# Linear attention and a four-expert mixture on one core: w1 in another row order, all its casts on POOL, and batches 0 and 1 in another order

## The chip, the cores and the metric

The kernel runs on one core of one Trainium2 chip. The time is that of the device, in microseconds (us), for one launch with inputs and outputs in HBM. Each kernel is launched several times and the median counts.

## The reference

All inputs are fp32. With q, k, v of shape [8 batches, 8 heads, 576 rows, 64], phi(x) = elu(x) + 1:

```python
q_p, k_p = (phi(q), phi(k))
kv = np.einsum('bhsd,bhse->bhde', k_p, v)
z = np.sum(k_p, axis=2)
num = np.einsum('bhsd,bhde->bhse', q_p, kv)
den = np.einsum('bhsd,bhd->bhs', q_p, z)[..., None] + 1e-06
x = (num / den).transpose(0, 2, 1, 3).reshape(4608, 512)
p = domain_probs / (domain_probs.sum(-1, keepdims=True) + 1e-09)    # [4608, 4]
for e in range(4):                      # w1[e]: [512, 1024], w2[e]: [1024, 512]
    h = np.maximum(x @ w1[e], 0.0)
    out += p[:, e:e + 1] * (h @ w2[e])
```

## The kernel before

The engines are PE (TensorE: matmuls and transposes), DVE (VectorE), ACT (ScalarE), POOL (GpSimd) and SP (SyncE, which issues nearly all DMAs). The order of the work on every engine, and of SP's DMAs, is written out by hand (`manual_schedule`): an engine does its instructions in the order in which the Python code emits them. SP's DMAs use eight semaphores in turn, so each issue waits until the eighth DMA before it has landed.

**Attention.** A batch is two head groups g of four heads. `load` brings one group of k, q or v (576 KB) into a `stage` tile; `exp` (ACT), `lin` and `phi` (DVE) make phi; `vcast` makes v fp16 (`vp`); `kv` multiplies phi(k) with v, and ACT copies the product to `kvz`; `qtr` transposes phi(q) on PE and `qcopy` brings it to `qT` (`qdma` does the same by a transposing DMA); `numden` multiplies and divides, giving `xs`; `xtr` transposes `xs` on PE and copies it to `xT` (`xdma`: by DMAs). `xT` holds x transposed, fp16, with its rows in the order (g, hh, a, d): of a group's four heads, head number 2a + hh.

**Mixture.** `moe_first` does the first 512 rows of x, expert by expert: eight products `ph` with w1 (L414, evicted by ACT, L421), then four products `py` with w2 (L427, scaled and added by DVE, L437 and L439). `moe_tile(i)`, i = 2 to 17, does 256 rows each; its second product takes seven products instead of eight from sums and differences of w2's quarters (`make_T` prepares them; `pB` holds the probabilities along the rows). In `moe_first` the work of batch 1, the loading of the later experts and the preparation hang on numbered slots, 12 for each expert: `at(h, 12 * e + fj, ...)` stands ahead of `ph` number fj, `12 * e + 8 + ns` ahead of `py` number ns.

**Weights.** w1 and w2 are loaded as fp32 in pieces of 512 KB into tiles that have another use later (`homes` gives their tags) and cast to fp16. A piece of w1 has 128 successive rows on the partitions, twice. `xT` wants another row order in which halves of 64 rows change places, so w1 is cast in pieces of 64 partitions by 512: the straight half on POOL (`cast_w1` with a = hh), the crossing half on ACT or DVE (`cross_w1`). Of w2's four pieces POOL casts two and DVE two.

**Probabilities.** `load_probs` has its two DMAs issued by POOL, behind the casts of w1(0) and w2(0) there; `norm_probs` normalizes (DVE), `turn_probs` transposes and writes them to DRAM (`p_rows`), from where `pB` is read.

**Order at the start.** SP: k, q, v of batch 0, then w1(0), w2(0), w1(1); in the slots w2(1), w1(2), w2(2), w1(3), batch 1's k, v, q, w2(3). Batch 0 goes through phi of k for both groups, then of q, before the products begin; `warmup` puts matmuls without use on PE.

Of the kernel before, what the change touches and what calls it, by code (L numbers as in the profile page):

```python
# [21 lines left out]
def kernel(  # L22
# [10 lines left out]
    nc = tc.nc  # L33

    B, H, S, D = q.shape
    N, E = moe_domain_probs.shape
    _, Dm, F = moe_w1.shape
# [9 lines left out]
    P = 128  # L47
    HP = P // 2
    CB = S // HP
    G = H // 4  # L50
    DC = Dm // P
    FC = F // P
    NT = 512
# [9 lines left out]
    CS = 5  # L63
# [14 lines left out]
    w1_sb = pw.tile([P, E, DC, F], FP16, tag="w1")  # L78
    w2_sb = pw.tile([P, E, FC, Dm], FP16, tag="w2")
    xT = pc.tile([P, DC, RC * HP], FP16, tag="xT")  # L80
    w1_src = moe_w1.rearrange("e (dc p) f -> e p dc f", p=P)
    w2_src = moe_w2.rearrange("e (fc p) d -> e p fc d", p=P)
    NTP = N // P
    p_raw = pc.tile([P, (2 * NTP + 1) * E], FP32, tag="praw")
# [23 lines left out]
    class Batch:  # L108
# [91 lines left out]
        def numden(self, g, part, where=None):  # L200

            c0, c1 = ((0, 6), (6, CB))[part]
            if part == 0:
                self.xs[g] = att([P, CB, 2, D], "xs")
            if where:
                nd = ppm.tile([P, NT], FP32, tag=where, bufs=3, name="nd").rearrange(
                    "p (k n) -> p k n", k=1
                )
            else:
                nd = ppa.tile([P, 2, NT], FP32, tag="aps", bufs=1, name="nd")  # L210
            for c in range(c0, c1):
                i = c - c0
                for hh in range(2):
                    rows = slice(hh * HP, (hh + 1) * HP)
                    nc.tensor.matmul(  # L215
                        out=nd[rows, i // 3, (i % 3) * 2 * DE : (i % 3 + 1) * 2 * DE],
                        lhsT=self.qT[g][:, c, rows],
                        rhs=self.kvz[g][:, hh, :],
                        start=True,
                        stop=True,  # L220
                    )
            nb = (c1 - c0) // 3
            view = nd[:, 0:nb, 0 : 6 * DE].rearrange("p k (m e) -> p k m e", e=DE)
            rc = pa.tile([P, 2, 6], FP32, tag="rc", bufs=4, name="rc")[:, 0:nb, :]
            nc.vector.tensor_scalar(
                rc, view[:, :, :, D : D + 1].rearrange("p k m o -> p k (m o)"),
                1e-6 * INV, None, AO.add,
            )
            nc.vector.reciprocal(rc, rc)
            nc.vector.tensor_tensor(  # L230
                out=self.xs[g][:, c0:c1, :, :].rearrange(
                    "p (k c) a d -> p k (c a) d", k=nb
                ),
                in0=view[:, :, :, 0:D],
                in1=rc.broadcast_to([P, nb, 6, D]),
                op=AO.mult,
            )
# [45 lines left out]
                    c += n  # L283


    staged = {}
    homes = iter(
        ("Ta",) * 3 + ("Tb",) * 3 + ("S",) * 2
        + ("chain", "pB", "wx") + ("Ta",) * 3 + ("stage",) * 2
        + ("stage",) * 4 + ("Tb",) * 3 + ("S",)  # L290
        + ("S", "chain", "pB", "wx") + ("Tb",) * 3 + ("S",)
    )
    BUFS = {"stage": 6, "Ta": 3, "Tb": 3, "S": 2, "chain": 1, "pB": 1, "wx": 1}

    def wstage(name):
        tag = next(homes)
        return pa.tile([P, 2, NT], FP32, tag=tag, bufs=BUFS[tag], name=name)

    def load_w1(e):
        for fh in range(2):  # L300
            for g in range(2):
                wr = wstage("wr")
                nc.sync.dma_start(
                    out=wr, in_=w1_src[e, :, 2 * g : 2 * g + 2, fh * NT : (fh + 1) * NT]
                )
                staged[1, e, fh, g] = wr
                for i in range(2):
                    cast_w1(e, fh, g, i, i, nc.gpsimd.tensor_copy)

    def cast_w1(e, fh, g, a, hh, copy):  # L310

        copy(
            out=w1_sb[a * HP : (a + 1) * HP, e, 2 * g + hh, fh * NT : (fh + 1) * NT],
            in_=staged[1, e, fh, g][hh * HP : (hh + 1) * HP, a, :],
        )

    def cross_w1(e, fh, copy):
        for g in range(2):
            for i in range(2):
                cast_w1(e, fh, g, i, 1 - i, copy)  # L320

    def load_w2(e):
        for i in range(4):
            wr = wstage("wr")
            nc.sync.dma_start(out=wr, in_=w2_src[e, :, 2 * i : 2 * i + 2, :])
            staged[2, e, i] = wr
            if i % 2 == 0:
                cast_w2(e, i, nc.gpsimd.tensor_copy)

    def cast_w2(e, i, copy):  # L330
        copy(out=w2_sb[:, e, 2 * i : 2 * i + 2, :], in_=staged[2, e, i])

    def load_probs():
        src = moe_domain_probs.rearrange("(b p c) e -> p b (c e)", b=B, c=CB)
        n = 2 * NTP * E
        for hh, at in ((0, E), (1, 0)):
            nc.gpsimd.dma_start(  # L337
                out=p_raw[hh * HP : (hh + 1) * HP, at : at + n].rearrange(
                    "p (b w) -> p b w", b=B
                ),  # L340
                in_=src,
            )
# [230 lines left out]
    def warmup(n, stat=None):  # L573
        pz = ppm.tile([P, NT], FP32, tag="mm", bufs=3, name="pz")
        for _ in range(n):
            nc.tensor.matmul(
                out=pz, lhsT=identh if stat is None else stat, rhs=warm, start=True, stop=True
            )
# [14 lines left out]
    nc.scalar.activation(warm[:, 0:1], identh[:, 0:1], AF.Exp)  # L593

    b0 = Batch(0)
    for src in (k, q, v):
        for g in range(G):
            b0.load(src, g)
    b0.vcast(0, gcopy, CS, CB)
    b0.vcast(1, gcopy, CS, CB)  # L600
    load_w1(0)
    load_w2(0)
    load_probs()
    load_w1(1)

    for g in range(G):
        b0.exp(k, g)
        b0.lin(k, g)
        b0.phi(k, g)
    warmup(6, b0.kp[0][:, 0, :, :].rearrange("p a d -> p (a d)"))  # L610
    b0.exp(q, 0)
    b0.lin(q, 0)
    b0.phi(q, 0)
    b0.exp(q, 1)
    b0.lin(q, 1)
    b0.phi(q, 1)
    b0.qtr(0, ("yy", "yy"))
    b0.vcast(0, scopy, 0, CS)
    b0.qtr(1, ("mm", "mm"))
    b0.kv(0)  # L620
    b0.qcopy(0, 0, vcopy)
    b0.qcopy(0, 1, vcopy)
    b0.vcast(1, vcopy, 0, CS)
    b0.qcopy(1, 0, scopy)
    b0.qcopy(1, 1, vcopy)
    b0.numden(0, 0)
    b0.kv(1, ("yy", "mm"))
    b0.numden(0, 1, "yy")
    cross_w1(0, 0, scopy)
    b0.numden(1, 0)  # L630
    b0.numden(1, 1, "mm")
    warmup(2)
    b0.xtr(0, (scopy, scopy))
    warmup(2)
    b0.xtr(1, (vcopy, scopy), ("yy", "yy"))

    def at(h, s, *fns):
        h.setdefault(s, []).extend(fns)

    def L(f, *args):  # L640
        return lambda: f(*args)
# [1 line left out]
    gps, dve = nc.gpsimd, nc.vector  # L643
    bt = Batch(1)
    h = {}
    at(h, 0, L(load_w2, 1), L(load_w1, 2), L(cross_w1, 0, 1, vcopy))
    at(h, 7, norm_probs)
    at(h, 12, L(load_w2, 2), L(load_w1, 3))
    at(h, 13, *[L(bt.load, s, g) for s in (k, v, q) for g in range(G)])
    at(h, 14, L(bt.vcast, 0, gcopy), L(bt.vcast, 1, gcopy), L(load_w2, 3))  # L650
    at(h, 18, turn_probs)
    for e in range(E):
        for i in (1, 3):
            at(h, 12 * e + 2 * i, L(cast_w2, e, i, vcopy))
    for s, e, fh in ((8, 1, 0), (10, 1, 1), (20, 2, 0), (22, 2, 1)):
        at(h, s, L(cross_w1, e, fh, scopy))
    at(h, 29, L(cross_w1, 3, 0, vcopy))
    at(h, 31, L(cross_w1, 3, 1, vcopy))
    at(h, 32, L(bt.exp, k, 0), L(bt.lin, k, 0))
    at(h, 33, L(bt.exp, k, 1), L(bt.phi, k, 0))  # L660
    at(h, 34, L(bt.lin, k, 1))
    at(h, 35, L(bt.phi, k, 1))
    at(h, 36, L(bt.kv, 0), L(bt.exp, q, 0), L(bt.lin, q, 0))
    at(h, 37, L(bt.phi, q, 0))
    at(h, 38, L(bt.kv, 1), L(bt.exp, q, 1), L(bt.lin, q, 1))
    at(h, 39, L(bt.qtr, 0), L(bt.qcopy, 0, 0, vcopy), L(bt.qcopy, 0, 1, vcopy))
    at(h, 40, L(bt.phi, q, 1), L(load_pB, 2))
    at(h, 42, L(bt.qtr, 1, ("yy", "yy")), L(bt.qcopy, 1, 0, vcopy), L(bt.qcopy, 1, 1, vcopy))
    at(h, 43, L(bt.numden, 0, 0))
    at(h, 44, L(bt.numden, 0, 1, "mm"))  # L670
    at(h, 45, L(bt.numden, 1, 0))
    at(h, 46, L(bt.numden, 1, 1, "mm"), L(bt.xtr, 0, (scopy, scopy)))
    at(h, 47, L(bt.xtr, 1, (scopy, scopy), ("mm", "mm")))
    for s, kind in zip((13, 14, 15, 16), (3, 1, 2, 4)):
        at(h, s, L(make_T, 0, kind, dve))
    at(h, 41, lambda: gcopy(out=after, in_=bt.qp[1][:, 0, 0, 0:1]))
    at(h, 41, *[L(make_T, 1, kind, gps) for kind in (3, 1, 2, 4)])
    at(h, 42, *[L(make_T, 2, kind, gps) for kind in (3, 1, 2, 4)])
    b2 = Batch(2)
    at(h, 48, *[L(b2.load, s, g) for s in (k, q, v) for g in range(G)])  # L680
    moe_first(h)
# [85 lines left out]
```

## Time and profile before

| | us |
|---|---|
| median of 3 runs | 529.11 (528.38 to 529.33) |
| profiled execution | 528.63 |
| its span | 526.9 |
| PE busy | 510.1 |
| DVE, ACT, POOL busy | 324.0, 190.2, 208.8 |
| first `ph` of `moe_first` begins | 19.72 |
| `moe_tile(2)` begins | 82.58 (on the chain of waits: 82.74) |

The profile is of one execution on the chip. Times in it are us from the start of the span, unless marked ns. "Busy" of PE contains pipelined matmuls, so that two of them may overlap. Windows give, for a stretch, each engine's busy time and number of instructions, the granted clock, the share of the 16 DMA engines' time and GB/s. The list of DMA issues gives a transfer's tile and source, its issuing queue, number, size, and the time from the issue to its landing. The granted clock was 0.999 of full speed.

### The profile page before, as it was taken

Reading aid. Unit: us, or ns where it says so; the run is one execution under the profiler, and the core shown is the slowest. Engines: PE = TensorE matmul, PEld = TensorE weight load, DVE = VectorE, ACT = ScalarE, POOL = GpSimd, SP = SyncE. Lnnn points to the kernel's source line nnn. Section 1 sums busy time; section 2 is a strip of 40 time slices with the busy share of each in tenths; the row PEclk is TensorE's granted clock in tenths of the full one; section 3 lists DMA queues with packets and bytes.
Section 4 is the critical chain, followed back from the end, with each engine's and each line's share of the span. In section 5 each row is a group of like instructions: output and inputs, shape, how many; then the busy total and the mean of one; then the engine's idle time right before and its main releaser. Section 6 shows DMA issues by size and latency. Waiting matters only on the chain.

```text
span 526.9 us, 11518 instructions
## 1 busy us (share of the span) xinstructions
PE 510.1 (97%) x4756; PEld 419.9 (80%) x4756; DVE 324.0 (61%) x669; ACT 190.2 (36%) x327; POOL 208.8 (40%) x193
## 2 busy tenths in 40 slices
PE   3889999999999999999999999999999999999996
PEld 1434457888888888888888888888888888888885
DVE  5655976877647674767377746765576545444443
ACT  5767543424341425143523433153413131313130
POOL 3768369324151605051423334241515060606060
PEclk9999999999999999999999999999999999999999
DMA  8999827356554137341923273524143202020301
GB/s 325 406 379 406 317 60 224 148 139 186 135 213 115 47 83 268 83 89 41 309 61 90 63 234 118 96 77 130 33 95 46 81 1 82 2 81 3 78 2 40
DMA packets 65330, 70.97 MB, mean 135 GB/s; under 512 B 31821, under 2 KB 40157, under 8 KB 65277
## 3 DMA queue, kind: packets, MB, share of 16 engines
q1 hardware_dynamic: 65180, 70.08, 42.9%
q8 instruction: 37, 0.61, 0.5%
q0 software_dynamic: 96, 0.15, 0.1%
q14 instruction: 17, 0.13, 0.1%
HBM read 53.62 MB, written 9.51 MB: 120 GB/s over the span
## 4 chain that ended last, share of the span: by engine, by line
PE 93%; DMA 5%; DVE 1%; POOL 0%; SPq 0%; issue 0%; DVEq 0%
PE ph L480 43%; PE px L515 16%; PE py L515 11%; PE pz L515 5%; PE pw L515 5%; PE py L427 4%; PE ph L414 4%; DMA wr<-in_moe_w_dram 2%; PE nd L215 2%; PE pk L167 2%; DMA st<-in_v_dram 2%; DMA p_raw<-in_moe_domain_probs_dram 1%; SPq L117 0%; POOL p_raw L337 0%; PE pq L187 0%; PE px L264 0%
## 5 line engine op out<-in xcount | busy, mean ns | idle before, releaser
L498 POOL TENSOR_TENSOR ga<-hr,pB 128x512 f16<-128x512 f16 x120 | 143.4, 1195 | 272.5 <-ACT hr L497 272.5
L480 PE MATMUL ph<-xT,w_sb 128*128 128x256 f16 x2048 | 232.5, 273 | 0.0
L480 PEld LDWEIGHTS <-w_sb 128*128 128x128 f16 x2048 | 197.4, 98 | 26.1
L492 DVE SCALAR_TENSOR_TENSOR ga<-ph,pB 128x512 f16<-128x512 f32 x136 | 94.0, 692 | 111.8 <-PE ph L480 111.4
L497 ACT ACTIVATE hr<-ph 128x512 f16<-128x512 f32 x120 | 71.6, 597 | 185.3 <-PE ph L480 184.1
L515 PEld LDWEIGHTS <-ga 128*128 128x128 f16 x1280 | 125.2, 98 | 14.5
L515 PEld LDWEIGHTS <-s 128*128 128x128 f16 x512 | 50.0, 98 | 5.9
L135 ACT ACTIVATE ee<-st 128x1152 f16<-128x1152 f32 x32 | 37.0, 1158 | 11.9 <-DMA st<-in_k_dram 10.3
L537 DVE TENSOR_TENSOR s<-ga 128x512 f16<-128x512 f16 x64 | 28.3, 482 | 15.8 <-POOL ga L498 15.8
L515 PE MATMUL pz<-w_sb,ga 128*128 128x256 f16 x256 | 30.6, 273 | 0.0
L515 PE MATMUL pw<-tw,ga 128*128 128x256 f16 x256 | 30.6, 273 | 0.0
L515 PE MATMUL py<-w_sb,s 128*128 128x256 f16 x256 | 30.6, 273 | 0.0
L515 PE MATMUL px<-tw,s 128*128 128x256 f16 x256 | 30.6, 273 | 0.0
L515 PE MATMUL px<-tw,ga 128*128 128x256 f16 x256 | 30.6, 273 | 0.0
L515 PE MATMUL px<-w_sb,ga 128*128 128x256 f16 x256 | 30.6, 273 | 0.0
L515 PE MATMUL py<-w_sb,ga 128*128 128x256 f16 x256 | 30.6, 273 | 0.0
L427 PE MATMUL py<-w_sb,ht 128*128 128x512 f16 x128 | 29.0, 379 | 1.6 <-DVE acc L437 1.6
L414 PE MATMUL ph<-xT,w_sb 128*128 128x512 f16 x128 | 29.2, 379 | 0.3 <-ACT xT L275 0.3
L528 DVE SCALAR_TENSOR_TENSOR res<-px,chain 128x256 f32<-128x256 f32 x32 | 12.1, 420 | 28.1 <-PE px L515 28.1
L142 DVE TENSOR_SCALAR tt<-st 128x1152 f16<-128x1152 f32 x32 | 25.1, 785 | 4.9 <-DMA st<-in_k_dram 4.9
L525 ACT ACTIVATE chain<-px 128x256 f32<-128x256 f32 x32 | 12.3, 383 | 42.2 <-PE px L515 42.2
L149 DVE TENSOR_TENSOR phi<-ee,tt 128x1152 f16<-128x1152 f16 x32 | 24.1, 754 | 2.1 <-ACT ee L135 1.3
(69 smaller groups left out, 376.5 us busy)
## 6 DMA issues: line engine op xcount, KB each, us to landing
wr<-in_moe_w_dram SPq DMA_DIRECT2D x32, 512.0 KB, 11.0
st<-in_k_dram SPq DMA_DIRECT2D x16, 576.0 KB, 6.4
st<-in_q_dram SPq DMA_DIRECT2D x16, 576.0 KB, 5.5
st<-in_v_dram SPq DMA_DIRECT2D x16, 576.0 KB, 8.7
pB<-p_rows SPq DMA_DIRECT2D x16, 512.0 KB, 3.9
out_dram<-res SPq DMA_DIRECT2D x64, 128.0 KB, 2.4
out_dram<-acc SPq DMA_DIRECT2D x8, 128.0 KB, 2.3
xT<-xs SPq DMA_TRANSPOSE x32, 2.6
```

Of the source, the lines that this page charges most:

```text
L135: nc.scalar.activation(self.ee[id(src), g][:, :, c0:c1, :], st[:, :, c0:c1, :], AF.Exp)
L142: nc.vector.tensor_scalar(self.tt[id(src), g][:, :, c0:c1, :], self.st[id(src), g][:, :, c0:c1, :], 0.0, 1.0, AO.max, AO.add,)
L149: nc.vector.tensor_tensor(out=self.dst(src, g)[:, c0:c1, :, :].rearrange("p c a d -> p a c d"), in0=self.ee[id(src), g][:, :, c0:c1, :], i ...
L414: nc.tensor.matmul(out=ph, lhsT=w1_sb[:, e, dc, fj * P : (fj + 1) * P], rhs=xT[:, dc, 0:NT], start=(dc == 0), stop=(dc == DC - 1),)
L427: nc.tensor.matmul(out=py, lhsT=hT[fj // FH][:, fj % FH, ns * P : (ns + 1) * P], rhs=w2_sb[:, e, fj, :], start=(fj == 0), stop=(fj == FC - 1),
L480: nc.tensor.matmul(out=ph[:, f, :], lhsT=w1_sb[:, e, dc, fj * P : (fj + 1) * P], rhs=xT[:, dc, cols], start=(dc == 0), stop=(dc == DC - 1),)
L492: nc.vector.scalar_tensor_tensor(out=to, in0=ph, scalar=0.0, in1=pb, op0=AO.max, op1=AO.mult)
L497: nc.scalar.activation(hr, ph, AF.Relu)
L498: nc.gpsimd.tensor_tensor(out=to, in0=hr, in1=pb, op=AO.mult)
L515: nc.tensor.matmul(out=to, lhsT=sts[e][:, f, :], rhs=movs[e][:, f, :], start=(start and e == 0 and f == 0), stop=(e == E - 1 and f == FH - 1),
L525: nc.scalar.activation(chain[:, n, :], src, AF.Copy, scale=OUTS)
L537: tt(out=S1[e], in0=a21[e], in1=a22[e], op=AO.add)
```

## The change

- w1 is loaded in the row order of `xT`: a transfer brings the 128 rows (a, d) of one (g, hh), with all 1024 columns (512 KB); for expert 0 in two parts of 512 columns (256 KB), the first columns of all four pieces first. The casts are whole (128 partitions), and all on POOL, as are w2's. `cross_w1` goes away.
- `load_probs` goes by SP's queue, between w1(0) and w2(0).
- Batch 0 is loaded in the order k0, q0, v0, q1, k1, v1 and worked off by head group. v's first group is cast whole by POOL.
- Batch 1's k and v are loaded ahead of the last w1, its q behind it. Its second group of q is transposed by DMA (`qdma`) instead of on PE, and its first group of x by DMAs (`xdma`) instead of on PE; its steps stand in somewhat earlier slots, `load_pB(2)` in a later one.
- `make_T` of expert 1 goes from POOL to DVE, in expert 2's slots.

```diff
@@ -200,7 +199,7 @@
         def numden(self, g, part, where=None):
 
             c0, c1 = ((0, 6), (6, CB))[part]
-            if part == 0:
+            if g not in self.xs:
                 self.xs[g] = att([P, CB, 2, D], "xs")
             if where:
                 nd = ppm.tile([P, NT], FP32, tag=where, bufs=3, name="nd").rearrange(
@@ -283,12 +282,11 @@
                     c += n
 
 
-    staged = {}
     homes = iter(
         ("Ta",) * 3 + ("Tb",) * 3 + ("S",) * 2
-        + ("chain", "pB", "wx") + ("Ta",) * 3 + ("stage",) * 2
-        + ("stage",) * 4 + ("Tb",) * 3 + ("S",)
-        + ("S", "chain", "pB", "wx") + ("Tb",) * 3 + ("S",)
+        + ("Ta",) * 3 + ("chain", "stage", "stage", "pB", "wx")
+        + ("Tb",) * 3 + ("S", "S", "chain", "pB", "wx")
+        + ("Tb",) * 3 + ("S", "S", "chain", "pB", "wx")
     )
     BUFS = {"stage": 6, "Ta": 3, "Tb": 3, "S": 2, "chain": 1, "pB": 1, "wx": 1}
 
@@ -296,45 +294,31 @@
         tag = next(homes)
         return pa.tile([P, 2, NT], FP32, tag=tag, bufs=BUFS[tag], name=name)
 
-    def load_w1(e):
-        for fh in range(2):
-            for g in range(2):
-                wr = wstage("wr")
+    w1_rows = moe_w1.rearrange("e (g a hh d) f -> e g hh a d f", g=G, a=2, hh=2)
+
+    def load_w1(e, parts=1):
+
+        n = F // parts
+        wr = [wstage("wr").rearrange("p a f -> p (a f)") for _ in range(DC)]
+        for part in range(parts):
+            cols = slice(part * n, (part + 1) * n)
+            for dc in range(DC):
                 nc.sync.dma_start(
-                    out=wr, in_=w1_src[e, :, 2 * g : 2 * g + 2, fh * NT : (fh + 1) * NT]
+                    out=wr[dc][:, cols], in_=w1_rows[e, dc // 2, dc % 2, :, :, cols]
                 )
-                staged[1, e, fh, g] = wr
-                for i in range(2):
-                    cast_w1(e, fh, g, i, i, nc.gpsimd.tensor_copy)
-
-    def cast_w1(e, fh, g, a, hh, copy):
-
-        copy(
-            out=w1_sb[a * HP : (a + 1) * HP, e, 2 * g + hh, fh * NT : (fh + 1) * NT],
-            in_=staged[1, e, fh, g][hh * HP : (hh + 1) * HP, a, :],
-        )
-
-    def cross_w1(e, fh, copy):
-        for g in range(2):
-            for i in range(2):
-                cast_w1(e, fh, g, i, 1 - i, copy)
+                nc.gpsimd.tensor_copy(out=w1_sb[:, e, dc, cols], in_=wr[dc][:, cols])
 
     def load_w2(e):
         for i in range(4):
             wr = wstage("wr")
             nc.sync.dma_start(out=wr, in_=w2_src[e, :, 2 * i : 2 * i + 2, :])
-            staged[2, e, i] = wr
-            if i % 2 == 0:
-                cast_w2(e, i, nc.gpsimd.tensor_copy)
-
-    def cast_w2(e, i, copy):
-        copy(out=w2_sb[:, e, 2 * i : 2 * i + 2, :], in_=staged[2, e, i])
+            nc.gpsimd.tensor_copy(out=w2_sb[:, e, 2 * i : 2 * i + 2, :], in_=wr)
 
     def load_probs():
         src = moe_domain_probs.rearrange("(b p c) e -> p b (c e)", b=B, c=CB)
         n = 2 * NTP * E
         for hh, at in ((0, E), (1, 0)):
-            nc.gpsimd.dma_start(
+            nc.sync.dma_start(
                 out=p_raw[hh * HP : (hh + 1) * HP, at : at + n].rearrange(
                     "p (b w) -> p b w", b=B
                 ),
@@ -593,46 +577,42 @@
     nc.scalar.activation(warm[:, 0:1], identh[:, 0:1], AF.Exp)
 
     b0 = Batch(0)
-    for src in (k, q, v):
-        for g in range(G):
-            b0.load(src, g)
-    b0.vcast(0, gcopy, CS, CB)
+    for src, g in ((k, 0), (q, 0), (v, 0), (q, 1), (k, 1), (v, 1)):
+        b0.load(src, g)
+    b0.vcast(0, gcopy)
     b0.vcast(1, gcopy, CS, CB)
-    load_w1(0)
+    load_w1(0, 2)
+    load_probs()
     load_w2(0)
-    load_probs()
     load_w1(1)
 
-    for g in range(G):
-        b0.exp(k, g)
-        b0.lin(k, g)
-        b0.phi(k, g)
-    warmup(6, b0.kp[0][:, 0, :, :].rearrange("p a d -> p (a d)"))
-    b0.exp(q, 0)
-    b0.lin(q, 0)
-    b0.phi(q, 0)
-    b0.exp(q, 1)
-    b0.lin(q, 1)
-    b0.phi(q, 1)
-    b0.qtr(0, ("yy", "yy"))
-    b0.vcast(0, scopy, 0, CS)
+    for src, g in ((k, 0), (q, 0), (q, 1)):
+        b0.exp(src, g)
+        b0.lin(src, g)
+        b0.phi(src, g)
+        if g == 0 and src is k:
+            warmup(6, b0.kp[0][:, 0, :, :].rearrange("p a d -> p (a d)"))
+        elif g == 0:
+            b0.qtr(0, ("yy", "yy"))
+            b0.qcopy(0, 0, vcopy)
+            b0.qcopy(0, 1, vcopy)
+    b0.kv(0)
+    b0.exp(k, 1)
+    b0.lin(k, 1)
+    b0.phi(k, 1)
     b0.qtr(1, ("mm", "mm"))
-    b0.kv(0)
-    b0.qcopy(0, 0, vcopy)
-    b0.qcopy(0, 1, vcopy)
-    b0.vcast(1, vcopy, 0, CS)
-    b0.qcopy(1, 0, scopy)
+    b0.qcopy(1, 0, vcopy)
     b0.qcopy(1, 1, vcopy)
+    b0.vcast(1, scopy, 0, CS)
     b0.numden(0, 0)
     b0.kv(1, ("yy", "mm"))
     b0.numden(0, 1, "yy")
-    cross_w1(0, 0, scopy)
+    b0.numden(1, 1, "mm")
     b0.numden(1, 0)
-    b0.numden(1, 1, "mm")
+    warmup(1)
+    b0.xtr(0, (scopy, scopy), ("yy", "yy"))
     warmup(2)
-    b0.xtr(0, (scopy, scopy))
-    warmup(2)
-    b0.xtr(1, (vcopy, scopy), ("yy", "yy"))
+    b0.xtr(1, (scopy, vcopy))
 
     def at(h, s, *fns):
         h.setdefault(s, []).extend(fns)
@@ -643,39 +623,31 @@
     gps, dve = nc.gpsimd, nc.vector
     bt = Batch(1)
     h = {}
-    at(h, 0, L(load_w2, 1), L(load_w1, 2), L(cross_w1, 0, 1, vcopy))
-    at(h, 7, norm_probs)
-    at(h, 12, L(load_w2, 2), L(load_w1, 3))
-    at(h, 13, *[L(bt.load, s, g) for s in (k, v, q) for g in range(G)])
-    at(h, 14, L(bt.vcast, 0, gcopy), L(bt.vcast, 1, gcopy), L(load_w2, 3))
+    at(h, 0, L(load_w2, 1), L(load_w1, 2))
+    at(h, 6, norm_probs)
+    at(h, 12, L(load_w2, 2), *[L(bt.load, s, g) for s in (k, v) for g in range(G)])
+    at(h, 12, L(bt.vcast, 0, gcopy), L(bt.vcast, 1, gcopy))
+    at(h, 13, L(load_w1, 3), *[L(bt.load, q, g) for g in range(G)], L(load_w2, 3))
     at(h, 18, turn_probs)
-    for e in range(E):
-        for i in (1, 3):
-            at(h, 12 * e + 2 * i, L(cast_w2, e, i, vcopy))
-    for s, e, fh in ((8, 1, 0), (10, 1, 1), (20, 2, 0), (22, 2, 1)):
-        at(h, s, L(cross_w1, e, fh, scopy))
-    at(h, 29, L(cross_w1, 3, 0, vcopy))
-    at(h, 31, L(cross_w1, 3, 1, vcopy))
+    for s, kind in enumerate((3, 1, 2, 4)):
+        at(h, 13 + s, L(make_T, 0, kind, dve))
+        at(h, 25 + s, L(make_T, 1, kind, dve))
     at(h, 32, L(bt.exp, k, 0), L(bt.lin, k, 0))
     at(h, 33, L(bt.exp, k, 1), L(bt.phi, k, 0))
     at(h, 34, L(bt.lin, k, 1))
-    at(h, 35, L(bt.phi, k, 1))
-    at(h, 36, L(bt.kv, 0), L(bt.exp, q, 0), L(bt.lin, q, 0))
-    at(h, 37, L(bt.phi, q, 0))
-    at(h, 38, L(bt.kv, 1), L(bt.exp, q, 1), L(bt.lin, q, 1))
-    at(h, 39, L(bt.qtr, 0), L(bt.qcopy, 0, 0, vcopy), L(bt.qcopy, 0, 1, vcopy))
-    at(h, 40, L(bt.phi, q, 1), L(load_pB, 2))
-    at(h, 42, L(bt.qtr, 1, ("yy", "yy")), L(bt.qcopy, 1, 0, vcopy), L(bt.qcopy, 1, 1, vcopy))
-    at(h, 43, L(bt.numden, 0, 0))
-    at(h, 44, L(bt.numden, 0, 1, "mm"))
-    at(h, 45, L(bt.numden, 1, 0))
-    at(h, 46, L(bt.numden, 1, 1, "mm"), L(bt.xtr, 0, (scopy, scopy)))
-    at(h, 47, L(bt.xtr, 1, (scopy, scopy), ("mm", "mm")))
-    for s, kind in zip((13, 14, 15, 16), (3, 1, 2, 4)):
-        at(h, s, L(make_T, 0, kind, dve))
+    at(h, 35, L(bt.phi, k, 1), L(bt.kv, 0))
+    at(h, 36, L(bt.kv, 1), L(bt.exp, q, 0), L(bt.lin, q, 0))
+    at(h, 38, L(bt.exp, q, 1), L(bt.phi, q, 0))
+    at(h, 39, L(bt.lin, q, 1), L(bt.qtr, 0), L(bt.qcopy, 0, 0, vcopy), L(bt.qcopy, 0, 1, vcopy))
+    at(h, 40, L(bt.phi, q, 1), L(bt.qdma, 1))
+    at(h, 41, L(bt.numden, 0, 0))
+    at(h, 42, L(bt.numden, 0, 1, "yy"))
+    at(h, 43, L(bt.xdma, 0))
+    at(h, 44, L(bt.numden, 1, 0), L(load_pB, 2))
+    at(h, 45, L(bt.numden, 1, 1, "mm"))
+    at(h, 46, L(bt.xtr, 1, (scopy, scopy)))
     at(h, 41, lambda: gcopy(out=after, in_=bt.qp[1][:, 0, 0, 0:1]))
-    at(h, 41, *[L(make_T, 1, kind, gps) for kind in (3, 1, 2, 4)])
-    at(h, 42, *[L(make_T, 2, kind, gps) for kind in (3, 1, 2, 4)])
+    at(h, 41, *[L(make_T, 2, kind, gps) for kind in (3, 1, 2, 4)])
     b2 = Batch(2)
     at(h, 48, *[L(b2.load, s, g) for s in (k, q, v) for g in range(G)])
     moe_first(h)
```

More of the change, by code (lines that the diff above doesn't have):

```diff
@@ L80 @@
     xT = pc.tile([P, DC, RC * HP], FP16, tag="xT")
-    w1_src = moe_w1.rearrange("e (dc p) f -> e p dc f", p=P)
     w2_src = moe_w2.rearrange("e (fc p) d -> e p fc d", p=P)
```

## The prediction

> **What bounds the kernel now.** I read the page first: busy shares, slices, costliest groups. TensorE is busy almost throughout.
>
> ```profile
> PE 510.1 (97%) x4756; PEld 419.9 (80%) x4756; DVE 324.0 (61%) x669; ACT 190.2 (36%) x327; POOL 208.8 (40%) x193
> PE   3889999999999999999999999999999999999996
> DMA  8999827356554137341923273524143202020301
> ```
>
> Only the first two slices (13 us each) have room on PE; in exactly those the DMA engines are full. So the change, which touches the time up to the end of batch 1, can shorten little, and can lengthen whatever it makes PE wait for. Next the chain of waits, first 100 us:
>
> ```profile
> 24.55 6.39 DMA p_raw<-in_moe_domain_probs_dram
> ...
> 32.85 0.76 DVE acc L437
> 33.66 1.89 PE py L427 x8
> ...
> 66.49 0.97 PE ph L414 x4
> ...
> 82.74 13.97 PE ph L480 x128
> ```
>
> After the head, the one gap is in front of 33.66: expert 0's fourth output tile waits for a free accumulator bank, the evictions wait for the probabilities, which POOL issued late. PE's waits put it at 1.6 us. From 33.66 on PE runs through; `moe_tile(2)` begins at 82.74, and everything behind that (444.1 us) is code that the change leaves alone. The question is when tile 2 can begin.
>
> Then the transfers, because w1's are re-cut. The windows of 5 us, and the issues between 54 and 68 us:
>
> ```profile
> 45.00:50.00 5.00, 5.00 (x25) 2.23 (x23) 2.07 (x4) 3.29 (x6) 3.84 (x6) 1.00 1.05 408
> ```
> ```profile
> wr<-in_moe_w_dram SPq DMA_DIRECT2D x1, 512.0 KB, 10.8
> pB<-p_rows SPq DMA_DIRECT2D x1, 512.0 KB, 4.6
> p_rows<-pT SPq DMA_DIRECT2D x1, 72.0 KB
> ```
>
> 408 GB/s at share 1.05 is sixteen engines working: 25.5 GB/s each. In the second fence `p_rows<-pT` alone has no time to landing. Its semaphore record says why: every other SP transfer adds sixteen counts as its data lands; this one adds one update as its issue ends, and twelve between 7.7 and 9.7 us after its start. Its outer dimension is 72 rows. So it ran on twelve engines, not sixteen; twelve is the largest number up to sixteen that divides 72. All other plain SP transfers here have outer dimensions of 64 or 128, and sixteen landings.
>
> [...]
>
> **Part 1, w1's transfers (decides).** Before, one reads [128 rows, 2, 512] into 128 partitions. After, the source is indexed `a` (2 halves, 128 rows apart), `d` (64 rows), columns. The two cannot be merged, as the step between halves is not 64 rows: the built program carries 2x64x512 (2x64x1024 for experts 1 to 3) against 128 partitions. The largest number that divides 2 and 128 is 2. By the `p_rows` row, w1 then runs on two engines, the same two each time, 64 partitions each.
>
> Price, per engine. A 256 KB part of w1(0) puts 128 KB on each: 131072 B / 25.5 GB/s = 5.15 us instead of 0.64. For w1(1) to w1(3) (4 KB rows) I use the packet records: 512, 1024 and 2048 B took 27, 46 and 84 ns, a line of 8 ns + B/26.95, so 4 KB takes 160 instead of 168 ns; 10.3 us becomes 9.9 per 512 KB.
> These two engines also carry their sixteenth of everything else, in SP's order. From v1's landing at 12.3: w1(0) 8 x 5.15 = 41.2; probabilities, 64 packets of 144 B at 13 ns, 0.9; w2(0) 4 x 1.29 = 5.15 (before's spacing); w1(1) 39.6; w2(1) 5.15; w1(2) 39.6; w2(2) 5.15; k, v of batch 1 4 x 1.45 = 5.8; w1(3) 39.6. The last w1 tile lands at 194.5, against 50.6 now. SP waits for the eighth transfer back before each issue, and for staging tiles that POOL frees 1.04 us after landing; walking both through, the two engines always have some 5 us or more queued, so I add nothing.
> [...]
>
> From there to tile 2: cast 1.04, eight `ph` groups 8 x 0.864, one `qtr` 0.6, two `nd` 0.75 make 9.3; PE has idled some 35 us, and the first matmuls of the trace took 0.457 each (six in 2.74) against 0.223 (32 in 7.13), so about 1.7 more: 11.0. Side by side, w2(3) lands at 194.5 + 2.9 (q) + 5.15 = 202.6, and q's transpose behind it some 2.5 later, +10.6: no longer. Then `nd` 0.46, four `py` groups 6.92, `nd` 0.29, `px` 0.5: tile 2 begins at 194.5 + 11.0 + 8.2 = 213.7. That is 131.0 later than 82.7.
>
> **Part 2, everything else.** While PE waits for w1(3) these cost nothing; without that wait they count:
> - Probabilities on SP ahead of w2(0) instead of behind POOL's casts: p_raw is there before its first use: -1.6. They delay w2(0) by 0.9, which has to be there at about 27 and now is at 24.3: nothing.
> - Casts: ACT loses 20 x 0.616, DVE 12 x 0.42 and 8 x 0.69; POOL goes from 32 x 0.69 + 8 x 1.08 = 30.7 to 8 x 0.61 + 28 x 1.04 = 34.0 us. PE never waits for a cast in this trace, and POOL needs 8.3 per expert against 10.3 for loading one: nothing, covered by the 10.3; without that cover, POOL's 1.35 (slowest cast) for 1.04 makes 10.8, 0.5 per expert.
> - Batch 0 by head group: in DVE's order the copies of q's first group now stand ahead of `lin`/`phi` of q1 and k1. They wait for `qtr(0)`, which is behind six warm-up matmuls until 9.65, so DVE resumes at about 10.1 with 0.85 + 1.5 + 1.5 + 0.85 + 4.45 = 9.15 to do, ends at 19.25 instead of 18.6, and the first `ph` starts 0.7 late: +0.7 (0 if the copies fit earlier, +1.5 if `qtr(1)` falls behind as well).
> - Batch 1: `qtr(1)` and `xtr(0)` leave PE: -0.50 - 0.61 = -1.1. Three transpose issues (2.6 to 2.9 us to landing) are put on SP ahead of `pB`, which then lands by about 79, needed at 83.6. Behind SP's wait for `phi` of q1 stand only xT of batch 1, pB and the stores. `qT` lands at about 72.2 where PE wants it at 72: 0 to 1.
> - `make_T(1)` goes from POOL (4 x 2.12) to DVE (4 x about 1.0), in the room that the casts leave: nothing.
> Sum without part 1: 0.7 - 1.6 - 1.1 = -2.0.
>
> **The sum.** 528.6 (profiled execution: span 526.9 plus 1.7 around it) + 131.0 = 659.6; the median shown, 529.1, lies 0.5 above that execution. I say 660. Part 2's gains do not come off: they lie ahead of the wait for w1(3), or inside its chain, where they are already counted.
>
> **Rivals.**
> A rival on the other side: the split follows the 128 destination partitions, so w1 stays on sixteen engines. For it: bytes, rows and destination are those of a transfer that has sixteen landings today. Against it: 72 rows gave twelve, so a dimension of the pattern decides, and here the source's outer one is 2. Time: 528.6 - 2.0 = 526.6. It decides only where all sixteen share: with eight, w1(3) would land at 12.3 + 10.3 + 29.7 + 22.2 (the rest of the queue) = 74.5, still late for PE, which wants it at 64; with sixteen it is there at 54.5.
> A second rival: sixteen engines, but the head loses more than the 2.7 won. The place is PE's pause of some 1.5 us ahead of `qtr(1)`, with one warm-up matmul instead of two before `xtr(0)`; if PE falls back to the 0.457 of its first matmuls, the first 16 of expert 0 cost 16 x 0.234 = 3.7 more. With +0.7 that is 4.4 - 2.7 = +1.7: 530.3. It decides from 2 us of slow matmuls on. Against it: PE pauses by 0.7 to 0.9 four times before 19.7 now, and still starts at 0.223.
> [...]
>
> **How the numbers follow.** Two engines 0.86, sixteen and faster 0.10, sixteen and a slow head 0.04. The measurement can tell 0.2% (1.1 us) from no change; the first case is slower by far, the second mostly faster, the third mostly slower: 0.09, 0.02, 0.89. Range: w1's 160 us may be off by a tenth either way, as no row shows two engines alone (26.95 GB/s would make 156, packets without overlap 166), so -15; upwards the same and up to 6 for a moment in which the two engines run dry or q's transpose lands late: 645 to 682. The cases near 527 are left out.
>
> **What would show it.** Right: `wr` of w1 with no landing time or some tens of us; DMA at a low share, about 50 GB/s, from 15 to 195 us; PE idle ahead of `ph` of each expert, waiting for POOL's cast or w1's DMA; tile 2 near 214 and the same 444 us behind it. Wrong: DMA share near 1 until 62 us and tile 2 near 80.6 (the first rival), or L414's first matmuls at 0.4 us each (the second). Two engines, but w1's 512 KB at clearly other than 9.9 us, would leave the mechanism and spoil the size.

## The result and the profile after

| | before | after |
|---|---|---|
| median, us | 529.3 (528.38 to 529.42, 5 runs) | 667.8 (667.05 to 669.35, 5 runs) |
| ratio of the runs, 95% interval | | 1.2624 [1.2603, 1.2644] |
| profiled execution, span | 528.6, 526.9 | 668.1, 666.3 |
| last piece of w1 has landed | 50.6 | 202.76 |
| `moe_tile(2)` begins (chain) | 82.74 | 222.33 |
| from there to the end of the span | 444.2 | 444.0 |

The last row says that nothing behind `moe_tile(2)` changed: all of the 139.4 us by which the span grew lies ahead of it. Two single runs beside the experiments fell far out, one of experiment 1 at 1367.85 and one of the kernel before at 672.26; the ratios leave them out. The page after has the same four lines to compare: PE's busy time, its slices, its granted clock and the DMA engines' slices (a slice is now 16.7 us).

```profile
PE 525.3 (79%) x4737; PEld 422.8 (63%) x4737; DVE 311.8 (47%) x651; ACT 176.5 (26%) x304; POOL 201.8 (30%) x183
PE   4337008109007999999999999999999999999997
PEclk9667558658657999999999999999999999999999
DMA  6123241263163829454174254336423421012111
```

PE now works less than half of the time in nine of the first twelve slices, and the DMA engines are far from full there: neither is busy, so something narrow stands between them. The group of `ph` names what PE waited for, the list of issues gives w1's and w2's pieces without any landing time (and all of SP's other transfers too, as w1's pieces went through all eight of its semaphores), and one window inside w1(1) shows how little moves:

```profile
L398 PE MATMUL ph<-xT,w_sb 128*128 128x512 f16 x128 | 43.6, 489 | 126.5 <-POOL w_sb L309 126.5
```
```profile
wr<-in_moe_w_dram SPq DMA_DIRECT2D x28, 512.0 KB
wr<-in_moe_w_dram SPq DMA_DIRECT2D x8, 256.0 KB
```
```profile
60.00:80.00 20.00, 6.64 (x30) 2.66 (x27) 4.56 (x7) 0.00 (x0) 2.07 (x2) 0.71 0.14 56
```

126.5 us of waiting for POOL's casts, while POOL itself worked 2.07 us of these 20. DMA share 0.14 of sixteen engines is two engines and a little; 56 GB/s is 2 x 25.5 plus as little. POOL's timeline shows what its casts waited for; the columns are start, duration, operation, and in brackets the idle time before it and its releaser:

```profile
68.82 1.04 POOL L309 CAST w_sb<-wr 128x1024 f16<-128x1024 f32 x1 [8.89 <-DMA wr<-in_moe_w_dram]
78.76 1.04 POOL L309 CAST w_sb<-wr 128x1024 f16<-128x1024 f32 x1 [8.90 <-DMA wr<-in_moe_w_dram]
89.41 1.04 POOL L309 CAST w_sb<-wr 128x1024 f16<-128x1024 f32 x1 [9.61 <-DMA wr<-in_moe_w_dram]
101.25 1.04 POOL L309 CAST w_sb<-wr 128x1024 f16<-128x1024 f32 x1 [10.80 <-DMA wr<-in_moe_w_dram]
```

The 512 KB pieces of w1(1) come 9.9, 10.7 and 11.8 us apart. So POOL is not slow; it waits for the transfers. The chain of waits says the same up to its last link ahead of tile 2:

```profile
150.32 52.44 DMA wr<-in_moe_w_dram x2
202.76 0.05 issue
202.81 1.05 POOL w_sb L309
203.86 0.05 issue
203.91 4.02 PE ph L398 x9
...
222.33 13.97 PE ph L464 x128
```

In the semaphore record each w1 transfer posts two landings besides the update at its issue: two engines. w2's pieces, between them, post sixteen.

### The profile page after: what moved, and what is told of

It reads as the page before. It is cut to its first block, busy times and chain, and to the rows that moved or that the text cites. A ratio compares the mean times of both kernels' runs of the same rounds, so it can differ in the third digit from the quotient of the medians.

```text
span 666.3 us, 11426 instructions
## 1 busy us (share of the span) xinstructions
PE 525.3 (79%) x4737; PEld 422.8 (63%) x4737; DVE 311.8 (47%) x651; ACT 176.5 (26%) x304; POOL 201.8 (30%) x183
## 4 chain that ended last, share of the span: by engine, by line
PE 69%; DMA 17%; SPq 13%; POOL 0%; issue 0%; DVE 0%
PE ph L464 34%; DMA wr<-in_moe_w_dram 17%; PE px L499 13%; PE py L499 8%; SPq L306 7%; PE pw L499 4%; PE pz L499 4%; SPq L314 4%; PE nd L214 2%; PE ph L398 1%; PE pk L166 1%; SPq L321 1%; PE py L411 1%; SPq L116 0%; POOL w_sb L309 0%
## 5 line engine op out<-in xcount | busy, mean ns | idle before, releaser
L464 PEld LDWEIGHTS <-w_sb 128*128 128x128 f16 x2048 | 197.5, 98 | 26.0
L398 PE MATMUL ph<-xT,w_sb 128*128 128x512 f16 x128 | 43.6, 489 | 126.5 <-POOL w_sb L309 126.5
L398 PEld LDWEIGHTS <-w_sb 128*128 128x128 f16 x128 | 14.3, 117 | 152.8 <-POOL w_sb L309 134.6
L309 POOL CAST w_sb<-wr 128x1024 f16<-128x1024 f32 (+1 forms) x20 | 17.3, 866 | 151.5 <-DMA wr<-in_moe_w_dram 151.5
L405 ACT ACTIVATE ht<-ph 128x512 f16<-128x512 f32 x32 | 19.1, 597 | 126.2 <-PE ph L398 126.2
```

The lines of the kernel that those rows point to most:

```text
L398: nc.tensor.matmul(out=ph, lhsT=w1_sb[:, e, dc, fj * P : (fj + 1) * P], rhs=xT[:, dc, 0:NT], start=(dc == 0), stop=(dc == DC - 1),)
L464: nc.tensor.matmul(out=ph[:, f, :], lhsT=w1_sb[:, e, dc, fj * P : (fj + 1) * P], rhs=xT[:, dc, cols], start=(dc == 0), stop=(dc == DC - 1),)
```

## Experiments

Theory: w1's transfers go over two engines, because 2 is the largest number that divides the outer dimensions of both sides, and this alone makes the kernel slower. Rivals: the order of the rows in HBM is slow to read; POOL's casts or the new order of the head hold PE up.

**1. Two transfers of 64 rows instead of one of 2 x 64.** The change, with each w1 piece cut so that its outer dimension is 64. The row order and POOL's casts stay.

```diff
-                nc.sync.dma_start(
-                    out=wr[dc][:, cols], in_=w1_rows[e, dc // 2, dc % 2, :, :, cols]
-                )
+                for a in range(2):
+                    nc.sync.dma_start(
+                        out=wr[dc][a * HP : (a + 1) * HP, cols],
+                        in_=w1_rows[e, dc // 2, dc % 2, a, :, cols],
+                    )
...
-    load_w1(0, 2)
+    load_w1(0)
```

> The changed kernel, but each w1 piece is fetched by two DMAs of 64 rows (one for each a), 256 KB each, so that both outer dimensions are 64; w1(0) is fetched with whole rows. All else of the change stays. Theory (the source's outer dimension of 2 confined w1 to two engines): w1 loads at about 400 GB/s again, the last w1 piece lands by about 56 instead of 202.8, PE no longer waits for L309, and the time is 529.3 - 2.0 = 527.3 by the sum of part 2 (526 to 528.5). Rival (the loss comes from the row order in HBM, from POOL as the only caster or from the order of the transfers on SP): the time stays above 600. Second rival (sixteen engines, but the slow head): about 531.

Measured: 541.06 (540.79 without the run that fell out), ratio to before 1.0231 [1.0205, 1.0257]. PE's wait for w1, and the transfers:

```profile
PE ph L400 <- POOL w_sb L311: 8.6, 8, 2.1
```
```profile
wr<-in_moe_w_dram SPq DMA_DIRECT2D x32, 256.0 KB, 10.6
```

The landing times are back, and 126.5 us of waiting have become 8.6. The two engines are the cause of nearly all of it, and neither POOL nor the row order is worth more than what is left. But that is still 13 to 14 us above the expected 527.3, and this was a miss. The window shows it, beside the 408 GB/s of before in the same stretch:

```profile
45.00:50.00 5.00, 5.00 (x25) 2.25 (x23) 0.90 (x2) 1.56 (x5) 2.69 (x3) 1.00 1.04 252
```

All sixteen engines are taken (share 1.04), and move little: a 4 KB packet took 272 ns in the mean, against 159 in the undisturbed parts of the changed kernel. Experiment 9 takes this up.

**2. The same with the old head,** to price batch 0's order (loading k, q, v for both groups and working them off as before).

> As e1_halves, with batch 0 loaded and worked off in the old order (without the crossing casts, which are not needed). In the changed kernel's trace the first ph began at 20.69 against 19.72 before. Theory (that order costs what the first ph is late): 1.0 below e1_halves, and 3.0 below the kernel before, 526.3. Rival (the head is covered by something that arrives later, weights or casts): within 0.3 of e1_halves.

Measured: 541.05, ratio 1.0229 [1.0208, 1.0250], the same as 1. PE waits for weights behind either head, so this priced nothing; experiment 8 does.

**3. w2's pieces held back.** In the changed kernel the loads of w1 were slower than 9.9 us at the end of each expert. Here only `homes` changes: w2(1) and w2(2), and the last piece of w1(1) and w1(2), all use the one `chain` tile, so that no w2 piece can move while w1(1) or w1(2) does. w1(3) is left as it was and is the control.

```diff
-        + ("Ta",) * 3 + ("chain", "stage", "stage", "pB", "wx")
-        + ("Tb",) * 3 + ("S", "S", "chain", "pB", "wx")
+        + ("Ta",) * 3 + ("chain",) * 5
+        + ("Tb",) * 3 + ("chain",) * 5
         + ("Tb",) * 3 + ("S", "S", "chain", "pB", "wx")
```

> The changed kernel, but w2(1) and w2(2) go through the one staging tile that the last piece of w1(1) and of w1(2) uses, so none of them is issued before that piece is cast. Read is the distance between the landings of w1's 512 KB pieces, which was 9.9, 10.6 and 11.8 within w1(1) in the changed kernel. Theory (pieces of w2 that the other fourteen engines move at full speed slow down the two engines' packets): 9.9 throughout w1(1) and w1(2), and the old 10 to 12.5 within w1(3), where q and w2(3) still run beside. Rival (the two engines run dry between pieces, because SP waits for slots or tiles): distances of 10.6 and more stay. The time itself rises by 10 to 30, as w2's pieces now go one by one.

Measured: 690.84 (one run; longer, as w2's pieces now come one after another, 4.6 us apart, behind w1's). POOL's casts of w1(2), and then of w1(3):

```profile
128.02 1.04 POOL L309 CAST w_sb<-wr 128x1024 f16<-128x1024 f32 x1 [9.62 <-DMA wr<-in_moe_w_dram]
137.96 1.04 POOL L309 CAST w_sb<-wr 128x1024 f16<-128x1024 f32 x1 [8.90 <-DMA wr<-in_moe_w_dram]
147.89 1.04 POOL L309 CAST w_sb<-wr 128x1024 f16<-128x1024 f32 x1 [8.90 <-DMA wr<-in_moe_w_dram]
157.82 1.04 POOL L309 CAST w_sb<-wr 128x1024 f16<-128x1024 f32 x1 [8.89 <-DMA wr<-in_moe_w_dram]
...
202.33 1.04 POOL L309 CAST w_sb<-wr 128x1024 f16<-128x1024 f32 x1 [8.90 <-DMA wr<-in_moe_w_dram]
213.49 1.04 POOL L309 CAST w_sb<-wr 128x1024 f16<-128x1024 f32 x1 [10.12 <-DMA wr<-in_moe_w_dram]
225.39 1.04 POOL L309 CAST w_sb<-wr 128x1024 f16<-128x1024 f32 x1 [10.87 <-DMA wr<-in_moe_w_dram]
```

With nothing beside it a piece takes 9.93 to 9.94 every time; the control still goes 9.9, 11.2, 11.9. So w1's transfers on two engines are slowed while the other fourteen move pieces of w2: in the changed kernel w1's packets take 189 to 207 ns in the mean instead of 159 while one of the pieces of w2(1) or w2(2) passes, and each such piece costs w1 some 0.6 us. The two engines do not run dry meanwhile: from 79 to 89 us, within the piece that took 10.7 us, two or more of w1's packets are under way in 99.9% of the time.

**4. The divisor, from the other side.** The kernel before, each w1 piece as 66 + 62 rows instead of 128. Of the numbers up to sixteen 11 is the largest that divides 66, and 2 the largest that divides 62; bytes, order and casts stay.

```diff
-                nc.sync.dma_start(
-                    out=wr, in_=w1_src[e, :, 2 * g : 2 * g + 2, fh * NT : (fh + 1) * NT]
-                )
+                for r in (slice(0, 66), slice(66, P)):
+                    nc.sync.dma_start(
+                        out=wr[r],
+                        in_=w1_src[e, r, 2 * g : 2 * g + 2, fh * NT : (fh + 1) * NT],
+                    )
```

> The kernel before, but each w1 piece is fetched in two DMAs of 66 and 62 rows instead of one of 128. Row order, casts and bytes are the old ones; no dimension of 2 is outermost. Theory (the number of engines is the largest one up to 16 that divides the outer dimension): 66 rows go on eleven engines and 62 rows on two, so a piece keeps the two engines busy for 62 x 0.080 + 12 x 0.080 = 5.9 instead of 1.29; the last w1 piece lands at about 123 plus some 5 to 10 for the slowed packets, tile 2 begins at about 150 to 160 and the time is 597 to 607. Rival (it was the two-dimensional source pattern of the change): sixteen engines stay in use and the time is 529 to 531.

Measured: 609.19 (two runs), ratio 1.152 [1.150, 1.154]; the 66 rows posted 11 landings, the 62 rows 2. The row counts alone, in a kernel without any of the change, make it 80 us slower; the same cut at 64 rows costs 14 (experiment 9). The 2 us above the expected range were not followed up.

**5 to 8. The rest of the change, put into the kernel before** with w1 left as it was: the probabilities (5), batch 1's new slots (6), both (7), both and batch 0 by head group (8).

```diff
# 5: load_probs between load_w1(0) and load_w2(0), and
-            nc.gpsimd.dma_start(
+            nc.sync.dma_start(
# 6: the change's slots 35 to 46
+    at(h, 40, L(bt.phi, q, 1), L(bt.qdma, 1))
+    at(h, 43, L(bt.xdma, 0))
...
# 8: the change's head
+    for src, g in ((k, 0), (q, 0), (v, 0), (q, 1), (k, 1), (v, 1)):
+        b0.load(src, g)
...
```

> The kernel before, with one part of the change alone: the two DMAs of the probabilities are issued by SP between w1(0) and w2(0) instead of by POOL behind its casts. Theory (the 1.6 us that PE waits for the first evictions is all there is to win, and 0.9 us later w2(0) costs nothing): 1.6 below the kernel before. Rival (w2(0) becomes what arrives last, with fourteen-microsecond-old slack used up): 0.5 below to 0.5 above it.

> The kernel before, with the change's slots of batch 1 alone (q's second group transposed by DMA, x's first group by DMAs, earlier steps, pB later); the order of the loads is the old one. Theory (the two groups of transposes leave PE and nothing waits): 1.1 below the kernel before. Rival (qT or pB by SP's queue comes late for PE): 0 to 2 above it.

> Both of these parts on the kernel before. Theory (they add up): 2.7 below it, about 526.2 to 526.5; it would be the fastest of all. Rival (one of them hides what the other wins): within 0.5 of the better of the two.

> e7 with batch 0 loaded and worked off by head group as in the change (with the crossing casts of w1(0) on ACT kept). Theory (the first ph comes 0.7 to 1.0 late and nothing later absorbs it): 0.7 to 1.0 above e7, and 1.7 to 2.0 below the kernel before, which is the sum of the prediction's part 2. Rival (the head is covered, as e1 and e2 were equal): the same as e7 within 0.2.

| | median | ratio to before (528.64) | us | expected |
|---|---|---|---|---|
| 5 probabilities | 528.51 | 0.9992 [0.9983, 1.0001] | -0.1 | -1.6 |
| 6 batch 1 | 527.08 | 0.9975 [0.9965, 0.9985] | -1.6 | -1.1 |
| 7 both | 526.68 | 0.9966 [0.9955, 0.9978] | -2.0 | -2.7 |
| 8 and the head | 527.64 | 0.9982 [0.9974, 0.9991] | -1.0 | -1.7 to -2.0 |

Batch 1 came out a little better than expected. By the medians the head costs 527.64 - 526.68 = 1.0, with 0.7 forecast; the two profiles do not show it (tile 2 begins at 81.81 in 7, whose profiled run is one of its slower ones, and at 81.58 in 8), so this price is not free of what follows. 7 lies within 0.4 of 6, as its rival had it. The probabilities missed; 5 lies in its rival's range, but PE does not wait for w2(0) in its profile, as that rival had it. The casts on POOL, the order of batch 1's loads and `make_T(1)` were not priced by themselves.

In 5's profile PE's 1.6 us in front of the fourth tile are gone, but they are lost again in the head. Warm-up matmuls, the first `ph`, before and then in 5:

```profile
16.27 0.60 PE L576 MATMUL pz<-warm,identh 128*128 128x512 f16 x2
...
19.72 7.13 PE L414 MATMUL ph<-xT,w_sb 128*128 128x512 f16 x32 [0.33 <-ACT xT L275]
```
```profile
18.00 1.04 PE L576 MATMUL pz<-warm,identh 128*128 128x512 f16 x2
...
21.21 7.12 PE L414 MATMUL ph<-xT,w_sb 128*128 128x512 f16 x32 [0.34 <-ACT xT L275]
```

The same two matmuls take 1.04 instead of 0.60, the 18 `kv` products ahead of them 1.16 instead of 0.70, and the first `ph` is 1.5 us later. By the records of the granted clock PE is at full speed from 9.88 on before, and only from 19.16 on in 5 (19.32 in 7). 5's twelve runs lie in two groups, three at 527.0 to 527.15 and nine at 527.9 to 528.95: as if the clock came up early in some and late in others; the profiled run is one of the nine. Experiment 10 tests that.

6 shows the same exchange. Its probabilities still come by POOL, yet its profile has no wait for them. The fourth tile before, then the first `ph` and the four tiles in 6:

```profile
33.66 1.89 PE L427 MATMUL py<-w_sb,ht 128*128 128x512 f16 x8 [1.63 <-DVE acc L437]
```
```profile
20.91 7.12 PE L414 MATMUL ph<-xT,w_sb 128*128 128x512 f16 x32 [0.34 <-ACT xT L275]
27.88 7.07 PE L427 MATMUL py<-w_sb,ht 128*128 128x512 f16 x32
```

The first `ph` is 1.2 us later than before (the records have PE at half clock from 13.89 to 17.31) and the probabilities are there 1.0 us earlier, so the wait of 1.6 us is gone without the change that was to remove it. That is why 5 and 6 do not add up. From the first `ph` to tile 2 the profiles have 63.0 us before, 61.2 in 5 and 60.2 in 6, in 7 and in experiment 10: behind the head the wait and the transposes are worth 2.8 together (2.7 forecast), and the rest of the difference lies in the head.

**9. What half the partitions cost.** The kernel before, each w1 piece as two transfers of 64 rows in natural order (experiment 4's edit with `slice(0, 64), slice(64, P)`). Sixteen engines by either account.

> The kernel before, with each piece of w1 written by two transfers of 64 rows each (rows 0 to 63, rows 64 to 127) in their natural order, instead of one of 128. Both halves have a row count that sixteen divides, so both theories expect all sixteen engines. Theory A: what cost the half transfers of e1_halves their 13 us is that each writes only 64 partitions. Then the packets of w1 here are slower too (median of a 2 KB packet 130 to 150 ns instead of 84), the loads move 240 to 300 GB/s while w1 is under way, the last weights land some 10 us later than before, and the time is 535 to 541. Theory B: it was the order in which x^T's rows are read from HBM (every other block of 64 rows). Then nothing is lost here: packets at 84 ns and 529 to 531.

Measured: 542.66, ratio 1.0250 [1.0222, 1.0278], 1.7 us above the range of the first theory and far from the rival. Two windows of this one kernel, the first while the 64-row pieces of w1 pass, the second while w2's 128-row pieces do:

```profile
45.00:50.00 5.00, 5.00 (x26) 2.38 (x24) 3.33 (x5) 3.31 (x7) 2.54 (x3) 1.00 1.07 243
22.50:25.00 2.50, 2.50 (x14) 1.08 (x12) 0.80 (x2) 1.70 (x4) 1.29 (x1) 1.00 1.05 403
```

Same engines, same share, same size of packet (2 KB), and 243 GB/s against 403. In the first, the median packet took 146 ns, in the second 84. So what held experiment 1 back (252 GB/s) comes with transfers of 64 rows to 64 partitions, and not with x^T's row order. The two measures agree to about a tenth: 243 GB/s by the window, and eight packets of 146 ns per engine for 256 KB make about 224 GB/s. The runs do not part the 64 partitions from the smaller size of such a transfer, 256 KB, and they do not show why it is slow.

**10. PE kept busy in the head.** Experiment 7 with seven more warm-up matmuls.

```diff
     b0.qtr(0, ("yy", "yy"))
+    warmup(4)
...
     b0.numden(0, 1, "yy")
+    warmup(3)
```

> e7_probs_batch1 with seven more warm-up matmuls in the head of the kernel, four behind batch 0's first quarter and three behind its first head group, so that PE does not idle long there. Theory: the 1 us that e5_probs and e7_probs_batch1 fell short of their sums is PE at half its clock in the head until about 20 us. With PE kept busy the granted clock stays at 1.0, the first ph comes near 19.7 to 20.2 instead of 21.6, and the median is 525.5 to 526.1, some 0.7 to 1.0 below e7_probs_batch1's 526.7, with its runs closer together. Rival: the clock falls back anyway, or the added matmuls (seven of 0.3 to 0.6 us) stand in the way of batch 0's own: 526.7 to 527.7.

Measured: 525.93 (six runs, four of them at 525.86 to 525.93), ratio 0.9939 [0.9924, 0.9955] to before's 528.95 beside it. The head:

```profile
15.09 0.82 PE L576 MATMUL pz<-warm,identh 128*128 128x512 f16 x3
15.85 0.70 PE L215 MATMUL nd<-kvz,qT 128*64 128x130 f16 x18
16.48 0.60 PE L576 MATMUL pz<-warm,identh 128*128 128x512 f16 x2
...
19.92 2.38 PE L414 MATMUL ph<-xT,w_sb 128*128 128x512 f16 x10 [0.34 <-ACT xT L275]
```

The granted clock is at full speed from 9.86, the 18 `nd` products take 0.70 (1.25 in 7), and the first `ph` begins 1.7 us earlier than in 7's profile. The theory's numbers came. One profile of each is all that shows the clock, and 7's two fastest runs (525.75 and 526.07) came as low without the added matmuls: these seem to make the early clock more frequent rather than to bring something new. The kernel before with the added matmuls alone was not run. This is the fastest version of the study, 3.0 us below the kernel before, and it has the change's probabilities and batch 1, but neither its w1 transfers nor its head.

## Why the prediction was right, point by point

- **Two engines.** Right. Ahead of the result one row stood for it, 72 rows with twelve landings; that an outer dimension of 2 on one side alone does the same was my estimate, shown by no run then. Now it is shown from both sides: the landings (two), experiment 1 (cut the dimension of 2 away, and 126.5 us of waiting become 8.6), experiment 4 (66 rows with 11 landings and 62 with 2, +80 us).
- **Their price alone.** Right: 256 KB parts came 5.12 us apart (5.15 forecast), 512 KB pieces 9.93 to 9.94 in experiment 3 (9.9; 160/168 of the 10.3 would have been 9.8, so the last tenth is luck), a 4 KB packet took 159 ns (160). w1(0) was there at 53.3 (53.5), w2(0) at 58.9 (59.6).
- **The mis-sized term.** "The two engines always have some 5 us or more queued, so I add nothing" was true of their queues and missed the neighbours. While the other fourteen move w2's or batch 1's pieces, w1's packets grow; a 512 KB piece took up to 12.6 instead of 9.9. w1(3) landed at 202.76, not 194.5: +8.3, about all of the 7.8 us between forecast and median. Experiment 3 showed it for w1(1) and w1(2); w1(3) kept its neighbours there.
- **From there to tile 2.** 19.2 forecast, 222.33 - 202.76 = 19.6 measured. That PE starts at its slow rate was in it: nine `ph` products in 4.02, 0.447 each.
- **Part 2.** As forecast, it played no part in the changed kernel. By itself batch 1 gave -1.6 (-1.1), the head cost 1.0 by the medians (0.7), and the probabilities gave 0.1 at the median and 1.5 in the three fastest runs, of which there is no profile. That the parts add up held only where the clock came up early (experiment 10: -3.0, with -2.7 forecast for these two); else a late head and the wait for the probabilities hide each other.
- **First rival (sixteen engines, 526.6).** Excluded. Experiment 1 shows too that cutting the transfers apart does not get there: sixteen engines that write 64 partitions at a time make 541.
- **Second rival (clock falls back in the head).** I dismissed it because PE pauses four times by 0.7 to 0.9 us in the head of the kernel before and still starts at 0.223. It does happen: in the changed kernel the records have PE at half clock from 17.12 to 20.54, and its first `ph` began 1.0 late, at 20.69 (how much of that is the clock and how much the 0.7 of batch 0's order was not parted). In the 3.4 us ahead of 17.12 PE's pauses were 0.82, 0.39 and 0.24 us, none longer than the 0.90 of the kernel before, whose clock stayed full; so the length of a pause alone does not tell the two heads apart. The fall-back just decides nothing behind a wait of 126.5 us. The records change at 17.12, 20.54 and 23.95, 3.41 us apart. Why a given head falls into the slow half was not settled; with more matmuls, in experiment 10's profile, it did not.
- **A slip that changed nothing.** Before, the DMA engines were full in the first five slices, and not in exactly the first two.

## What to carry to other kernels

Before re-cutting a transfer, write down the outermost dimension of both sides as they reach the queue, and the partitions that one transfer writes: 128 rows as 2 x 64 ran on two engines, and as two times 64 on sixteen at 243 to 252 GB/s instead of 403 to 408. A DMA share of a few sixteenths while PE waits (0.14 here), and landing times that are missing from the list of issues, are the signs to look for; which transfer it is, the count of landings in the semaphore record says (2 for w1, 16 for w2). A gain of 1 or 2 us that is won behind the head can be lost again in it, if PE's clock comes up a few us later (19.16 instead of 9.88 in experiment 5); in experiment 10 a few useless matmuls in the pauses went with an early clock (9.86).

## What the runs showed of the hardware that was not expected

- Two engines slow down while the other fourteen work: 4 KB packets 159 ns alone, 189 to 207 in the mean beside a piece of w2.
- Sixteen engines writing 64 partitions at a time: 2 KB packets 146 ns instead of 84, 243 instead of 403 GB/s.
- With the same order of PE's work in the head, the clock was full from 9.9 us (before) or only from 19.2 us (experiment 5), and the first `ph` 1.5 us later.
